# Cached GQA attention block: K turned by VectorE in 32x32 blocks, V as the moving operand, row sums by row

## The chip, the cores and the metric

The kernel runs on one core of one Trainium2 chip. The metric is device time in microseconds (us), from one launch of the whole program. A core has TensorE (PE; its weight loads are a row of their own, PEld), VectorE (DVE), ScalarE (ACT), GpSimd (POOL), SyncE (SP), which here only issues DMAs, and 16 DMA engines that all queues share.

## The reference

There are 8 batches of 4 tokens, 32 query heads over 8 key heads, 2048 cached keys for each, 128 numbers to a head, and 512 to a token. All tensors are bf16.

```python
q = (x @ wq).reshape(B, Sq, Hq, Dh).transpose(0, 2, 1, 3)
k = jnp.repeat(k_cache, rep, axis=1)      # rep = 4 query heads for a key head
v = jnp.repeat(v_cache, rep, axis=1)
scores = jnp.einsum("bhqd,bhkd->bhqk", q, k) * (Dh ** -0.5)
p = softmax(scores)
o = jnp.einsum("bhqk,bhkd->bhqd", p, v)
return o.transpose(0, 2, 1, 3).reshape(B, Sq, Hq * Dh) @ wo
```

K and V are 33.6 MB each, wq and wo 4.2 MB each: nearly all of the traffic is read once.

## The kernel before

**Units.** The work is cut into 16 units, one for each batch and each half of the key heads: four key heads (G = 4), each with 16 query rows (4 heads by 4 tokens). A unit's K is one transfer of 2 MB (`load_k`, L93) and its V another (`load_v`, L101). In SBUF a head has 32 partitions (S = 32), and each partition holds 64 consecutive keys (C = 64 chunks of 128 numbers).

**One unit's steps.**
- `transpose_part` (L168), four times a unit: PE turns 8 blocks of 128x128 fp32 words (a word is a pair of bf16 numbers) into PSUM, and DVE (parts 0 and 3) or ACT (1 and 2) copies them to the tile kt.
- `scores` (L238): 8 matmuls for each half of the keys, with q (tile q_bd) as weights of 32 columns, so that four column groups of the array work side by side.
- `maxima` (L252): DVE's maximum of each row, a shuffle that exchanges the two halves of a row, and `less`, the negated larger one.
- `exponentials` (L271): ACT's exp of the scores to s_sb, with the sum of each row in l_sb.
- `probs_to_keys` (L282): DVE turns s_sb in 32x32 blocks (tile p_t); four POOL copies, one for each key head, spread p_t into the block form `probs`, of which there are two buffers (PB = 2).
- `norms`, `sums`, `inverses` (L303 to L327), every second unit: the row sums go through a matmul with ones, and DVE takes the reciprocal of 128x128.
- `values` (L331), four quarters: 64 matmuls with V as weights (128x128) and 64 columns of probs moving, summed in one PSUM tile.
- `finish` (L344): DVE multiplies by the reciprocal and writes oT, where the head's numbers lie on partitions.

**Head and tail.** At the start q is projected: both halves (L195 to L211), then both are spread into q_bd (L212 to L230). After the last unit `to_tokens` and `to_wo_rows` bring oT to the row order in which wo was loaded, and `project` adds 32 rows of wo for each partition. wo's buffer is wq's, and it is loaded at the end, save for 256 rows (`load_wx`, L109) that come earlier in two small transfers to wx_sb; `project_few` adds them.

**Order.** The order on every engine is the order in which the program emits the instructions (`manual_schedule`). The loop (L441) runs over steps n, in which unit n's K is turned and scored, unit n-1's probabilities are spread, and unit n-2's values are computed (LAG = 2): the turn's four parts come with the spread between them, then half of the values, scores, maxima, exponentials, and the other half. K and V have three buffers each (KB, VB). SP's queue holds the loads in one order (K of a unit, then V of two units before), and each waits for its buffer: K's for the last transpose that reads it, V's for the last value matmul.

Of the kernel before, what the change touches and what calls it, by code (L numbers as in the profile page):

```python
# [14 lines left out]
def kernel(  # L15
# [23 lines left out]
    NT, J = 4, C // 8  # L39
    HP = 8  # L40
    WR = 8
    XE, XR = 4, 8
    XP, XN = 64, 2 * XE * 4 * XR
    MR = WR - XN // 128
    NP = Hq // HP
    NW = MR + (NP - 1) * WR
# [7 lines left out]
    assert Dh == 128 and C == 64 and J == 8 and HQ == 16 and NU == 16 and T == 32  # L54
# [10 lines left out]
    psum_k = ctx.enter_context(tc.tile_pool(name="psum_k", bufs=2, space=bass.MemoryType.PSUM))  # L65
    psum_s = ctx.enter_context(tc.tile_pool(name="psum_s", bufs=1, space=bass.MemoryType.PSUM))
    psum_o = ctx.enter_context(tc.tile_pool(name="psum_o", bufs=1, space=bass.MemoryType.PSUM))
    psum_l = ctx.enter_context(tc.tile_pool(name="psum_l", bufs=1, space=bass.MemoryType.PSUM))

    order = ctx.enter_context(tc.manual_schedule())  # L70

# [4 lines left out]
    q_bd = const.tile([128, Hkv // G, 2, G, B, 2, HQ], BF16, name="q_bd")  # L76
    probs = [const.tile([128, C // 2, G, HQ, 2], BF16, name=f"probs{i}") for i in range(PB)]
    ident = const.tile([128, 128], BF16, name="ident")
    ident4 = const.tile([128, 128], FP32, name="ident4")
    ones = const.tile([128, 128], FP32, name="ones")  # L80
    by_gq = const.tile([128, G, HQ], FP32, name="by_gq")
    oT = [const.tile([128, HP, 2, B, Sq], BF16, name=f"oT{n}") for n in range(2)]
    oP = [const.tile([128, MR + WR, T], BF16, name="oP0"), const.tile([128, WR, 2, T], BF16, name="oP1")]
    oX = const.tile([XP, XR, T], BF16, name="oX")
    wx_sb = const.tile([XP, XR, D], BF16, name="wx_sb")
    nat_sb = const.tile([2 * T, XP * XR + HP * 128 - XN], BF16, name="nat_sb")
# [22 lines left out]
    def load_wx(h):  # L109
        few = XN // 2  # L110
        rows = wo[h * few : (h + 1) * few, :].rearrange("(b a r) j -> a b (r j)", a=XE, r=XR)
        q0 = h * XP // 2
        nc.sync.dma_start(wx_sb[q0 : q0 + 4 * XE, :, :].rearrange("q r j -> q (r j)"), rows)

    def load_wo(p, r0, n):
        if p == 0:
            rows = wo[XN : HP * 128, :].rearrange("(q r) j -> q r j", r=MR)
        else:
            rows = wo[p * HP * 128 : (p + 1) * HP * 128, :].rearrange("(q r) j -> q r j", r=WR)
        w0 = first_row(p) + r0  # L120
        nc.sync.dma_start(wo_sb[:, w0 : w0 + n, :], rows[:, r0 : r0 + n, :])

    def first_row(p):
        return 0 if p == 0 else MR + (p - 1) * WR
# [5 lines left out]
    for u in range(2, NU + 2):  # L130
        if u < NU:
            loads.append(("k", u))
        loads.append(("v", u - 2))
        if u in (6, 12):
            loads.append(("w", u // 12))
    loads.reverse()

    def load_ready(nk, nv):
        while loads:
            kind, u = loads[-1]  # L140
            if kind == "w":
                load_wx(u)
            elif u >= (nk + KB if kind == "k" else nv + VB):
                return
            else:
                (load_k if kind == "k" else load_v)(u)
            loads.pop()

    load_ready(0, 0)

    make_identity(nc, ident4[:])
    make_identity(nc, ident[:])
    nc.vector.memset(q_bd[:, :, :, :, :, :, :], 0.0)
    for pr in probs:
        nc.gpsimd.memset(pr[:, :, :, :, :], 0.0)  # L155
    nc.gpsimd.memset(ones[:, :], 1.0)
    nc.gpsimd.memset(wx_sb[:, :, :], 0.0)
    nc.gpsimd.memset(nat_sb[:, :], 0.0)
    nc.vector.tensor_reduce(
        out=by_gq[:, :, :],  # L160
        in_=ident4[:, :].rearrange("p (g c q) -> p g q c", g=G, c=2),
        axis=AX,
        op=ADD,
    )

    kt = {}

    def transpose_part(u, t):  # L168

        k4 = ks[u][:, :, :].rearrange("s c d -> s (c d)").bitcast(FP32)  # L170
        if t % 2 == 0:
            kt[(u, t // 2)] = ktpool.tile([128, 2 * J, 128, 2], BF16, tag="kt", name="kt")
        kp = psum_k.tile([128, J, 128], FP32, tag="k", name="kp")
        for j in range(J):
            w = (t * J + j) * 128
            nc.tensor.transpose(kp[:, j, :], k4[:, w : w + 128], ident4[:, :])  # L176
        j0 = (t % 2) * J
        (nc.scalar.copy if t in (1, 2) else nc.vector.tensor_copy)(  # L178
            out=kt[(u, t // 2)][:, j0 : j0 + J, :, :].rearrange("k j s e -> k (j s e)"),
            in_=kp[:, :, :].rearrange("k j s -> k (j s)").bitcast(BF16),  # L180
        )

    for t in range(NT):
        transpose_part(0, t)

    xtp = psum_o.tile([128, R, T], BF16, tag="o", name="xtp")
# [5 lines left out]
    q_nats = []  # L194
    for hq in range(Hkv // G):  # L195
        psq = psum_k.tile([128, rep * Dh], FP32, tag="k", name="psq")
# [10 lines left out]
        q_nat = small.tile([128, rep, 2, 2, Dh // 2], BF16, tag="p_t", name="q_nat")  # L207
        halves = psq[:, :].rearrange("t (h k e) -> t h e k", h=rep, e=2)
        nc.scalar.mul(out=q_nat[:, :, :, 0, :], in_=halves, mul=scale)  # L209
        nc.vector.tensor_scalar_mul(out=q_nat[:, :, :, 1, :], in0=halves, scalar1=scale)  # L210
        q_nats.append(q_nat)  # L211
    for hq in range(Hkv // G):  # L212
        for e in range(2):
            pse = psum_k.tile([128, rep, G, B, Sq], FP32, tag="k", name="pse")
            for h in range(rep):
                nc.tensor.matmul(  # L216
                    pse[:, h, :, :, :].rearrange("d g b s -> d (g b s)"),
                    lhsT=q_nats[hq][:, h, e, :, :].rearrange("t c k -> t (c k)"),
                    rhs=ident[:, :],
                    start=True,  # L220
                    stop=True,
                )
            for c in range(2):
                rows = slice(c * 64, (c + 1) * 64)
                (nc.scalar.copy if c else nc.vector.tensor_copy)(
                    out=q_bd[rows, hq, e, :, :, c, :].rearrange(
                        "d g b (h s) -> d (g b) h s", h=rep
                    ),
                    in_=pse[rows, :, :, :, :].rearrange("d h g b s -> d (g b) h s"),
                )  # L230

    wo_sb = wpool.tile([128, NW, D], BF16, tag="w", name="wo_sb")
# [5 lines left out]
    def scores(u, tp):  # L238
        hq, b = units[u]
        if tp == 0:  # L240
            s_pss[u] = psum_s.tile([128, 2, 2 * J, S], FP32, tag="s", name="s_ps")
        for e in range(2):
            for g in range(G):
                nc.tensor.matmul(  # L244
                    s_pss[u][g * 32 : (g + 1) * 32, tp, :, :],
                    lhsT=q_bd[:, hq, e, g, b, :, :],
                    rhs=kt[(u, tp)][:, :, g * S : (g + 1) * S, e],
                    start=(e == 0),
                    stop=(e == 1),
                )  # L250

    def maxima(u):  # L252
# [5 lines left out]
            in_=s_pss[u][:, :, :, :].rearrange("q t j s -> q (t j s)"),  # L258
            axis=AX,
        )  # L260
        nc.vector.stream_shuffle(swapped[:, :], top[:, :], [i ^ HQ for i in range(32)])
# [9 lines left out]
    def exponentials(u):  # L271
        s_sbs[u] = small.tile([128, 2 * J, S, 2], BF16, tag="s_sb", name="s_sb")
# [9 lines left out]
    def probs_to_keys(u):  # L282
        p_t = small.tile([128, 2 * J * 2, HQ, 2], BF16, tag="p_t", name="p_t")
        nc.vector.transpose(  # L284
            p_t[:, :, :, :].rearrange("s x q j -> s (x q j)").bitcast(FP32),
            s_sbs[u][:, :, :, :].rearrange("q a s j -> q (a s j)").bitcast(FP32),
        )
        by_gpsimd = nc.gpsimd.tensor_copy
        copies = [by_gpsimd] * G
        if u == NU - 1:  # L290
            copies = [nc.vector.tensor_copy, nc.vector.tensor_copy, nc.scalar.copy, by_gpsimd]
        for g in reversed(range(G)):
            rows = slice(g * S, (g + 1) * S)
            to = probs[u % PB][rows, :, g, :, :].rearrange("s x q j -> s x (q j)")
            of = p_t[rows, :, :, :].rearrange("s x q j -> s x (q j)")
            if copies[g] == nc.vector.tensor_copy:
                to, of = to.bitcast(FP32), of.bitcast(FP32)
            copies[g](out=to, in_=of)  # L298

    w_gqs = {}  # L300
    r_sbs = {}

    def norms(u):  # L303
        w_gqs[u] = small.tile([128, 2, NQ], FP32, tag="w_gq", name="w_gq")
        for i in range(2):
            nc.vector.tensor_scalar_mul(  # L306
                out=w_gqs[u][:, i, :],
                in0=by_gq[:, :, :].rearrange("k g q -> k (g q)"),
                scalar1=l_sbs[u + i][:, 0:1],
            )  # L310

    def sums(u):
        l_ps = psum_l.tile([128, 2 * NQ], FP32, tag="l", name="l_ps")
        nc.tensor.matmul(  # L314
            l_ps[:, :],
# [212 lines left out]
```

## Time and profile before

| | |
|---|---|
| time, 3 runs | 188.5 us median (187.68 to 192.32) |
| time of the profiled execution | 187.17 us |
| its span, first to last instruction | 185.2 us |
| mean granted PE clock | 0.962 of full speed |
| busy: PE, DVE, ACT, POOL | 134.7, 97.5, 89.1, 76.2 us |
| DMA traffic | 75.84 MB, 410 GB/s over the span |
| K transposes on PE (L176) | 512, 69.7 us busy |
| their copies (L178) | 32 on ACT of 1868 ns, 32 on DVE of 1225 ns |
| copies to probs on POOL (L298) | 61 of 1039 ns |
| DVE transposes to p_t (L284) | 16 of 706 ns |

A row of groups gives line, engine, operation, output and inputs, shape, count, then busy time and mean duration, and the idle time before with what ended it. A row of the timeline starts with the start and the duration in us; in brackets stands the idle time before it and the instruction that ended it. Busy shares are means over the whole span: what a step is worth is read from what ends the last wait there. Times of matmuls are pipelined, so a group's duration in the timeline says more than the mean of one.

### The profile page before, as it was taken

What the parts mean: (1) busy time and instruction counts of PE and PEld (TensorE: products, weight loads), DVE (VectorE), ACT (ScalarE), POOL (GpSimd) and SP (SyncE); (2) the same over time, 40 slices, a digit from 0 to 9 for tenths busy, and PEclk for the clock granted to TensorE, in tenths of its full rate; (3) what the DMA queues carried; (4) which work ended last, traced back from release to release, by engine and by line L of the source; (5) the groups of instructions that cost most, each with busy time, mean ns of one, the idle gap of its engine ahead of it and who ended that gap; (6) DMA issues with size and microseconds to landing.
All of it is one profiled execution on the core that took longest, in us unless ns stands there. A gap on an engine that the chain in (4) does not pass through costs nothing.

```text
span 185.2 us, 4496 instructions
## 1 busy us (share of the span) xinstructions
PE 134.7 (73%) x1982; PEld 107.2 (58%) x1982; DVE 97.5 (53%) x168; ACT 89.1 (48%) x78; POOL 76.2 (41%) x74
## 2 busy tenths in 40 slices
PE   0192969669798988976786869488878686876871
PEld 0192338358686767764665667467756474655750
DVE  4022177396477738746663657445845566366300
ACT  2034244663938466393637364573737363634100
POOL 8990000817346281735262608071535335352000
PEclk9998556999999999999999999999999999999999
DMA  6999999999999999999999999999999999999980
GB/s 191 481 418 393 435 432 425 428 439 428 428 425 428 439 412 435 428 425 435 432 419 435 428 428 430 425 442 414 435 425 428 435 425 432 425 428 411 425 321 14
DMA packets 6107, 75.84 MB, mean 410 GB/s; under 512 B 712, under 2 KB 808, under 8 KB 1576
## 3 DMA queue, kind: packets, MB, share of 16 engines
q1 hardware_dynamic: 6040, 75.55, 96.2%
q8 instruction: 15, 0.25, 0.5%
q14 instruction: 4, 0.03, 0.0%
q10 hardware_dynamic: 48, 0.02, 0.0%
HBM read 75.53 MB, written 0.03 MB: 408 GB/s over the span
## 4 chain that ended last, share of the span: by engine, by line
DMA 60%; PE 19%; ACT 11%; DVE 5%; issue 2%; SPq 0%; ACTq 0%
DMA k_sb<-in_k_cache_dram 38%; PE kp L176 10%; DMA x_sb<-in_x_dram 9%; DMA v_sb<-in_v_cache_dram 8%; ACT kt L178 8%; DMA wo_sb<-in_wo_dram 6%; PE s_ps L244 4%; DVE top L256 3%; PE o_ps L336 3%; ACT s_sb L274 2%; PE psq L200 2%; DVE kt L178 1%; PE pse L216 1%; DVE less L262 0%; DVE q_nat L210 0%
## 5 line engine op out<-in xcount | busy, mean ns | idle before, releaser
L298 POOL COPY probs<-p_t 32x1024 bf16<-32x1024 bf16 x61 | 63.4, 1039 | 92.9 <-DVE p_t L284 90.4
L176 PE MATMUL kp<-ident,k_sb 128*128 128x128 f32 x512 | 69.7, 288 | 35.2 <-DMA k_sb<-in_k_cache_dram 20.3
L176 PEld LDWEIGHTS kp<-ident,k_sb 128*128 128x128 f32 x512 | 58.8, 147 | 44.4 <-issue 21.4
L178 ACT COPY kt<-kp 128x2048 bf16<-128x2048 bf16 x32 | 58.1, 1868 | 21.5 <-PE kp L176 21.5
L178 DVE COPY kt<-kp 128x2048 bf16<-128x2048 bf16 x32 | 39.2, 1225 | 47.3 <-PE kp L176 47.1
L274 ACT ACTIVATE s_sb<-s_ps,less 128x1024 bf16<-128x1024 f32 x16 | 22.4, 1400 | 49.4 <-DVE less L262 49.4
L336 PEld LDWEIGHTS <-v_sb 128*128 128x128 bf16 x1024 | 33.4, 97 | 8.7 <-issue 6.7
L336 PE MATMUL o_ps<-probs,v_sb 128*128 128x64 bf16 x1024 | 35.7, 192 | 2.0 <-DMA v_sb<-in_v_cache_dram 1.6
L256 DVE TENSOR_REDUCE top<-s_ps 128x1 f32<-128x1024 f32 x16 | 19.6, 1225 | 12.2 <-PE s_ps L244 12.2
L244 PE MATMUL s_ps<-kt,q_bd 128*32 128x512 bf16 x256 | 17.9, 396 | 0.8 <-DVE kt L178 0.8
L284 DVE STREAM_TRANSPOSE p_t<-s_sb 128x512 f32<-128x512 f32 x16 | 11.3, 706 | 1.9 <-ACT s_sb L274 1.5
L325 DVE RECIPROCAL r_sb<-l_ps 128x128 f32<-128x128 f32 x8 | 7.7, 958 | 3.5 <-PE l_ps L314 3.4
L244 PEld LDWEIGHTS <-q_bd 128*32 128x32 bf16 x256 | 4.2, 96 | 7.1 <-DVE kt L178 5.5
L155 POOL MEMSET probs<- 128x4096 bf16 x2 | 7.0, 3512 | 0.0
L423 PE MATMUL out_ps<-wo_sb,oP 128*32 128x256 bf16 x60 | 4.3, 273 | 1.4 <-DMA wo_sb<-in_wo_dram 1.4
L346 DVE TENSOR_TENSOR oT<-o_ps,r_sb 128x64 bf16<-128x64 f32 x16 | 3.5, 216 | 2.3 <-PE o_ps L336 2.3
L423 PEld LDWEIGHTS <-oP 128*32 128x32 bf16 x60 | 2.9, 96 | 2.4 <-issue 2.2
L314 PE MATMUL l_ps<-w_gq,ones 128*128 128x128 f32 x16 | 3.2, 281 | 1.3 <-DVE w_gq L306 1.3
L209 ACT ACTIVATE q_nat<-psq 128x512 bf16<-128x512 f32 x2 | 1.2, 597 | 6.2 <-PE psq L200 6.2
L200 PE MATMUL psq<-wq_sb,xT_sb 128*32 128x512 bf16 x32 | 3.6, 629 | 0.3 <-DVE xT_sb L193 0.3
L262 DVE TENSOR_SCALAR less<-swapped,top 128x1 f32<-128x1 f32 x16 | 3.4, 214 | 0.6
L216 PE MATMUL pse<-ident,q_nat 128*128 128x128 bf16 x16 | 2.4, 302 | 1.7 <-DVE q_nat L210 0.9
(45 smaller groups left out, 46.3 us busy)
## 6 DMA issues: line engine op xcount, KB each, us to landing
k_sb<-in_k_cache_dram SPq DMA_DIRECT2D x16, 2048.0 KB, 22.2
v_sb<-in_v_cache_dram SPq DMA_DIRECT2D x15, 2048.0 KB, 25.6
wq_sb<-in_wq_dram SPq DMA_DIRECT2D x1, 4096.0 KB, 17.0
wo_sb<-in_wo_dram SPq DMA_DIRECT2D x2, 1024.0 KB, 21.1
v_sb<-in_v_cache_dram SPq DMA_DIRECT2D x1, 1536.0 KB
wo_sb<-in_wo_dram SPq DMA_DIRECT2D x4, 256.0 KB, 17.8
wo_sb<-in_wo_dram SPq DMA_DIRECT2D x1, 768.0 KB, 17.1
v_sb<-in_v_cache_dram SPq DMA_DIRECT2D x1, 512.0 KB, 15.7
```

Of the source, the lines that this page charges most:

```text
L155: nc.gpsimd.memset(pr[:, :, :, :, :], 0.0)
L176: nc.tensor.transpose(kp[:, j, :], k4[:, w : w + 128], ident4[:, :])
L178: (nc.scalar.copy if t in (1, 2) else nc.vector.tensor_copy)(out=kt[(u, t // 2)][:, j0 : j0 + J, :, :].rearrange("k j s e -> k (j s e)"), ...
L200: nc.tensor.matmul(psq[g * T : (g + 1) * T, :], lhsT=xT_sb[:, r, :], rhs=wq_sb[:, r, c0 : c0 + rep * Dh], start=(r == 0), stop=(r == R - 1),)
L244: nc.tensor.matmul(s_pss[u][g * 32 : (g + 1) * 32, tp, :, :], lhsT=q_bd[:, hq, e, g, b, :, :], rhs=kt[(u, tp)][:, :, g * S : (g + 1) * S, ...
L256: nc.vector.reduce_max(out=top[:, :], in_=s_pss[u][:, :, :, :].rearrange("q t j s -> q (t j s)"), axis=AX,)
L274: nc.scalar.activation(out=s_sbs[u][:, :, :, :].rearrange("q a s j -> q a j s"), in_=s_pss[u][:, :, :, :].rearrange("q t (a j) s -> q (t a ...
L284: nc.vector.transpose(p_t[:, :, :, :].rearrange("s x q j -> s (x q j)").bitcast(FP32), s_sbs[u][:, :, :, :].rearrange("q a s j -> q (a s j ...
L298: copies[g](out=to, in_=of)
L325: nc.vector.reciprocal(r_sb[:, :], l_ps[:, :])
L336: nc.tensor.matmul(o_pss[u][:, :], lhsT=vs[u][:, 2 * (2 * a + j) + c, :], rhs=probs[u % PB][:, 2 * a + c, :, :, j].rearrange("s g q -> s ( ...
L423: nc.tensor.matmul(out_ps[half * T : (half + 1) * T, :], lhsT=left, rhs=right[:, half * DH : (half + 1) * DH], start=first, stop=last,)
```

## The change

K is no longer turned by PE. VectorE turns it, half a unit (128 partitions by 2048 words) at a time, in blocks of 32x32 words, straight from k_sb to kt. The 128 numbers of a head then stay in blocks of 32 words, and q is spread to match: for each block column k and number e of a pair, q_bd holds weights of 64 columns (four heads by 16 query rows), which are zero where head and partition don't meet. The scores of a half are 8 matmuls of 512 columns on two column groups of 64.

The exchange of halves is two copies of 64 partitions in place of the shuffle. p_t goes to probs in eight copies of 32x512 elements, four on ACT and four on POOL. The sums stay by row: two POOL copies exchange the halves, POOL adds them (`total`), and VectorE takes the reciprocal of 128x1, for every unit. The values have the probabilities of two chunks as weights and 256 numbers of V moving: 32 matmuls a unit. ACT divides them by row (`divide`), a small fp32 matmul adds the two halves and turns them (`finish`), and ACT copies the result to oT. The PSUM pools become two buffers each for scores, values and the rest. In the head, one half of q is projected, scaled and spread before the other half is begun. wo is loaded whole at the end, with no rows before, and the last part comes in pieces of 4, 2 and 2 rows.

The loop's order is new too. The core of the diff:

```diff
+    def turn_keys(u, t):
+        kts[(u, t)] = ktpool.tile([128, CT, 2, S, 2], BF16, tag="kt", name="kt")
+        nc.vector.transpose(
+            kts[(u, t)][:, :, :, :, :].rearrange("k c h s e -> k (c h s e)").bitcast(FP32),
+            ks[u][:, t * CT : (t + 1) * CT, :].rearrange("s c d -> s (c d)").bitcast(FP32),
+        )
...
+    for hq in range(Hkv // G):
+        project_q(hq)
+        spread_q(hq)
...
+    def scores(u, t):
...
+        for i in range(4):
+            k, e = i // 2, i % 2
+            for h in range(2):
                 nc.tensor.matmul(
+                    s_pss[u][h * NQ : (h + 1) * NQ, t, :, :],
+                    lhsT=q_bd[:, hq, k, e, b, :, :].rearrange("k g q -> k (g q)"),
+                    rhs=kts[(u, t)][:, h * CT // 2 : (h + 1) * CT // 2, k, :, e],
+                    start=(i == 0),
+                    stop=(i == 3),
                 )
+    def swap_halves(engine, out, in_):
+        for h in range(2):
+            engine.tensor_copy(
+                out=out[h * NQ : (h + 1) * NQ, :], in_=in_[(1 - h) * NQ : (2 - h) * NQ, :]
+            )
...
     def probs_to_keys(u):
...
+        for h in range(2):
+            for g in range(G):
+                quad = 2 * h + g // 2
+                (nc.gpsimd.tensor_copy if g % 2 else nc.scalar.copy)(
+                    out=probs[u % PB][g * S : (g + 1) * S, h, :, :, g, :],
+                    in_=p_t[quad * S : (quad + 1) * S, :, g % 2, :, :].rearrange(
+                        "s x q j -> s x j q"
+                    ),
+                )
+    def inverses(u):
...
+        swap_halves(nc.gpsimd, swapped, l_sbs[u])
+        nc.gpsimd.tensor_tensor(out=total[:, :], in0=l_sbs[u][:, :], in1=swapped[:, :], op=ADD)
+        nc.vector.reciprocal(r_sbs[u][:, :], total[:, :])
     def values(u, quarter):
...
+        t, h = quarter // 2, quarter % 2
+        for a in range(CT // 4):
+            c = quarter * C // 4 + 2 * a
             nc.tensor.matmul(
+                o_pss[u][:, :, :].rearrange("n j d -> n (j d)"),
+                lhsT=probs[u % PB][:, h, t * CT // 4 + a, :, :, :].rearrange(
+                    "s j g q -> s (j g q)"
+                ),
+                rhs=vs[u][:, c : c + 2, :].rearrange("s c d -> s (c d)"),
+                start=(c == 0),
+                stop=(c == C - 2),
+            )
+    def divide(u):
...
+            nc.scalar.mul(
+                out=o_scs[u][rows, :], in_=o_pss[u][rows, h, :], mul=r_sbs[u][rows, 0:1]
             )
     def finish(u):
...
+        nc.tensor.matmul(o_t[:, :], lhsT=o_scs[u][:, :], rhs=both[:, :], start=True, stop=True)
+        nc.scalar.copy(
...
     for n in range(NU + LAG):
         w = n - LAG
+        if 0 < n < NU:
+            turn_keys(n, 0)
         if 0 < n <= NU:
             probs_to_keys(n - 1)
+            inverses(n - 1)
         if n < NU:
             scores(n, 0)
+            if n > 0:
+                turn_keys(n, 1)
+        if w >= 1:
+            finish(w - 1)
+        if n < NU:
             scores(n, 1)
             maxima(n)
             exponentials(n)
...
         if w >= 0:
+            for quarter in range(4):
+                values(w, quarter)
+            divide(w)
```

## The prediction

> **What bounds the kernel now.** I read the page first: the span, the slices, then the costliest groups.
>
> ```profile
> span 185.2 us, 4496 instructions
> PE 134.7 (73%) x1982; PEld 107.2 (58%) x1982; DVE 97.5 (53%) x168; ACT 89.1 (48%) x78; POOL 76.2 (41%) x74
> PEclk9998556999999999999999999999999999999999
> DMA  6999999999999999999999999999999999999980
> ```
>
> The DMA row is full from the second slice to the last but one. No engine is: 75.5 MB at 425 to 435 GB/s set the time, and the engines fit inside. The timeline of one steady unit says how well they fit:
>
> ```profile
> 150.26 0.70 DVE L284 STREAM_TRANSPOSE p_t<-s_sb 128x512 f32<-128x512 f32 x1
> 151.10 4.32 POOL L298 COPY probs<-p_t 32x1024 bf16<-32x1024 bf16 x4 [5.89 <-DVE p_t L284]
> 153.62 1.05 PE L244 MATMUL s_ps<-kt,q_bd 128*32 128x512 bf16 x16
> 154.72 1.23 DVE L256 TENSOR_REDUCE top<-s_ps 128x1 f32<-128x1024 f32 x1 [0.72 <-PE s_ps L244]
> 156.18 0.21 DVE L262 TENSOR_SCALAR less<-swapped,top 128x1 f32<-128x1 f32 x1
> 156.49 1.40 ACT L274 ACTIVATE s_sb<-s_ps,less 128x1024 bf16<-128x1024 f32 x1 [3.13 <-DVE less L262]
> 157.37 1.94 PE L176 MATMUL kp<-ident,k_sb 128*128 128x128 f32 x16 [1.64 <-DMA k_sb<-in_k_cache_dram]
> ```
>
> The same p_t step is at 159.62 one unit later, so a unit takes 9.7 us here, and the next unit's first matmul waits 1.64 us for K's DMA. Early on, with K there ahead, the chain of waits shows units 8.1 us apart (VectorE's maximum at 44.85, 52.96, 61.06). So this kernel's engines have 1.6 us to spare in each unit. POOL's four copies begin 0.14 us after p_t and take 4.3 us, but nothing on VectorE waits for POOL. That is what the change alters.
>
> **The loop after the change.** It removes 512 fp32 transposes of PE (69.7 us), their 64 evictions (58.1 us on ACT, 39.2 on DVE), the sums on PE and 16 matmuls of the extra wo rows, all under the DMA today. It adds 32 transposes of 128x2048 words on VectorE. Its queue now reads: first half of K's turn, p_t, the reciprocal, second half of the turn, maximum, two swaps, less. The reciprocal waits for POOL's total, and POOL does four copies to probs, two swaps and the addition first, the copies starting only after p_t. So VectorE stands at the reciprocal for POOL's whole leg; behind it stand the second turn, for it the second half of the scores, and for those the next maximum. I go round once, from the end of a unit's scores (us):
> - maximum to less: 0.06 to the start, 1.23 (L256), two swaps 0.30 (the shuffle of 128x1 takes 0.15), less 0.21, two gaps of 0.04: 1.88.
> - first turn. The nearest row is p_t: 512 words in 0.706. Not shown is 2048. The line through p_t and the maximum (1024 words in 1.225) rises by 1.01 ns a word and gives 2.26; four times p_t is 2.82; with the slope of POOL's memset (4096 in 3.51, 0.86 ns each) it is 2.03. I take 2.31, just over the line, since p_t is the same operation. 0.03 + 2.31, to 4.22. ACT's exponential (1.40 + 0.18) ends at 3.6, under it.
> - p_t 0.03 + 0.71: 4.96.
> - POOL: 0.14 to the start, then four copies of 32x512. 1024 elements take 1.04; half is 0.52, and the instruction's price at worst is not halved, 1.04. I take 0.56, by elements and a little fixed cost: 2.24, to 7.34. ACT makes the other four copies beside them (1.04 for 1024, so 0.6 each).
> - two swaps and an addition of one element on POOL: no such row; its shortest memsets take 0.11 and the 128-element select 0.295. 0.35 to 0.9 for the three; I take 0.55, to 7.89. Back to DVE 0.10, reciprocal of one element 0.20 (128 take 0.96): 8.19.
> - second turn 0.03 + 2.31: 10.53.
> - half the scores: eight matmuls of 512 columns, two column groups at once, so four in a row. Four groups of four in a row took 1.05 above and, at the granted clock of 0.5, 1.90 (the 16 at 26.55 in the head). PE would be idle some 4 us before this step, and the head shows what that does:
>
> ```profile
> 14.00:16.00 2.00, 1.09 (x8) 0.86 (x8) 0.66 (x1) 1.92 (x2) 0.00 (x0) 1.00 0.83 360
> 16.00:18.00 2.00, 0.00 (x0) 0.00 (x0) 0.56 (x1) 0.00 (x0) 0.00 (x0) 0.90 0.95 401
> 18.00:20.00 2.00, 1.28 (x16) 0.65 (x20) 0.22 (x1) 0.00 (x0) 0.00 (x0) 0.50 0.99 426
> 30.00:32.00 2.00, 2.00 (x13) 1.82 (x12) 1.64 (x3) 1.70 (x3) 0.00 (x0) 0.69 1.06 442
> ```
>
> (Columns: busy PE, PEld, DVE, ACT, POOL; then granted clock, DMA share, GB/s.) PE's last matmul ended at 15.3; a clock of 0.90 over 16 to 18 means half speed from about 17.6; it came back only near 31, after five unbroken busy us. So this half of the scores costs 1.05 to 1.90, or 3.4 if the two groups also don't overlap. I take 1.65, nearer the slow end: 12.2 with the 0.06 before it.
>
> One unit is 12.2 us (10.7 with every term low, 15.7 with every term high), so the DMA, at 9.7, is no longer the bound: K and V wait for buffers, which VectorE and PE free late. The new values (32 matmuls of 256 columns) run right after the scores: L423's 24 matmuls of 256 columns in pairs took 1.64, so 0.137 each, and the scores' slope of 0.215 per 512 gives 0.107: 3.4 to 4.4 at full clock, some 5.5 when they start at half. p_t ends at 4.96 and POOL's second pair of copies, which needs them done, starts at 6.2, so they are covered; beyond 6.2 each 0.1 counts.
>
> **Head.** x still lands at 18.4; the first xT copy ends at 18.97. The first projection's 16 matmuls end at 20.9 (half of L200's 3.6). Then four scalings in a chain, DVE and ACT in turn at 0.69 and 0.60 (L210, L209): 23.8. Four spreads of 0.6 with two PSUM buffers and copies of 0.58 to 0.69 (L225): the buffer is free at 26.6. Only then the second projection (1.8), its scalings (2.9) and spreads (2.6): 34.05. Two halves of the first scores at half clock, 3.6: 37.6. Before, they ended at 28.4. K0's turn, 4.6 us after its landing at 8.6, is hidden under x, and so are POOL's memsets (7.0 for probs, by size 3.5 for the two q_g), done near 12. The old order, both projections first and spreads after, had no such chain.
>
> **Tail.** After unit 15's scores: values of 13 to 5.0, their division (two ACT copies of some 0.28) and the fp32 matmul to 6.0; values of 14 to 9.9, division and matmul to 10.9; values of 15 to 14.6, division, matmul and copy to 15.8. Tokens, copies and row turns (8 + 8 small matmuls, 0.63, 0.58, 0.68, 0.43 in the old tail, with the first projection of 1.1 between) to 18.3; 48 matmuls at 0.068 to 21.7; copy 0.37; then 3.3, as from 181.9 to the old end: 25.8 with gaps. wo has landed by then: V15's buffer comes free one unit earlier, and 15 us of transfers follow it. The 256 wo rows that went in two transfers of 0.13 MB between K and V (SP's queue, L113) now go with the rest: 0.6 us of transfer, moved from one place to another and covered in both.
>
> **Sum.** 37.6 + 15 x 12.2 + 25.8 = 246.4 of span. The profiled run took 187.17 for a span of 185.2, so 2.0 more: 248.4 against its 187.2, forecast 248. The median of the runs shown is 188.5, 0.7% above the profiled one, less than my terms are sure of. The unit's ends give 226 and 301 by the same sum.
>
> **Rivals.**
> - *The clock stays low through the values too.* For: 4 to 5 us of idleness in each unit, and the head's slow recovery. Against: scores and values in one piece are over 5 us busy. Scores 1.90, values 6.9 (32 x 0.213), and POOL's second pair waits 0.75: 13.2 a unit, 37.6 + 198 + 26.5 + 2.0 = 264.
>
> The Trainium skill (TensorE: Matmul & The Clock Gate, Part 1: The HAM clock gate) says half clock follows an idle window of some 3.4 us and full clock a busy one of as much. The trace shows half clock sooner, 2.3 us after the last matmul, and a later return. By the page's figure for the return the values would warm up half-way, which is the forecast, not this rival.
>
> - *POOL's copies cost by instruction,* 1.04 each for half the elements: 14.1 a unit, 277. Against: its memsets go with size.
> - *POOL's leg doesn't hold VectorE* (total is ready when asked for): 12.2 - 3.03 = 9.2 a unit, 37.6 + 138 + 25.8 + 2.0 = 203. Against: copies stand ahead of the swaps in POOL's queue.
> - *VectorE keeps up, not slower.* Place: the same wait at the reciprocal. If it is gone and turns (2.03) and scores (1.05) sit at their low ends, a unit is 8.0 and the DMA is the bound again. It decides from about 8.3 a unit, where the late start is caught up. K4 is asked for at 43 to 45, when the earlier transfers end at about 42; K15 lands 2 us later than before's 157.3, its scores end 6.6 later, 24 of tail: 190 + 2.0 = 192.
>
> **How the numbers follow.** Forecast 0.62 (own range 232 to 262), low clock 0.14, POOL's price 0.10, no hold 0.08, keeps up 0.06. Range 218 to 274: it leaves out the last two and most of POOL's price, about 0.2. Two per cent is about what a measurement of this kernel tells from no change: the DMA alone needs today's time, so faster 0.02 and same 0.04, both out of the last rival; slower 0.94.
>
> **What would show it.** Right: VectorE idle some 3 us before each reciprocal, ended by POOL; turns of 2.3 us; maxima 12 us apart; DMA slices of 7 or 8 tenths; first scores ending near 37; PEclk below 9 in the loop. Wrong: turns near 1.2, idle at the reciprocal below 1 us, or DMA slices still full. Over 13 us a unit, the clock and POOL's copies are to be read first.

## The result

The changed kernel takes 250.6 us (median of 4 runs, 250.0 to 252.1); the kernel before took 188.1 us beside it. The ratio is 1.3365, 95% interval 1.3285 to 1.3444. Some runs on these chips are disturbed and some 2 to 4% longer; ratios here compare undisturbed runs alone. The profiled execution took 250.01 us for a span of 248.2.

The page of the kernel after, its span, engines and DMA row:

```profile
span 248.2 us, 2569 instructions
PE 144.5 (58%) x964; PEld 91.0 (37%) x964; DVE 117.7 (47%) x140; ACT 86.2 (35%) x160; POOL 59.1 (24%) x124
PEclk9999996555968778968778867768867768877999
DMA  7999999397998979998979998979997909199500
```

The DMA row has holes from the eighth slice on, and no engine is above 58%. So neither the transfers nor any engine's amount of work looks like the bound: the loop waits within itself. The chain of work that ended last, read in order of time over one unit, says where (start, duration in us, what; steps of under 0.1 us are left out):

```profile
122.04 1.93 PE s_ps L209 x8
124.00 1.24 DVE top L227
125.25 0.15 DVE swapped L219
125.42 0.16 DVE swapped L219
125.60 0.21 DVE less L233
125.81 2.22 DVE kt L139
128.03 0.60 DVE p_t L255
...
128.78 0.60 POOL probs L262
...
130.73 0.62 POOL probs L262
131.40 0.18 POOL l_swapped L219
131.62 0.19 POOL l_swapped L219
131.88 0.20 POOL l_total L276
132.11 0.16 DVE r_sb L277
132.27 2.22 DVE kt L139
134.53 1.88 PE s_ps L209 x8
136.44 1.24 DVE top L227
```

Every step begins within 0.15 us of the end of the one before it. One unit is a single file: PE, VectorE, POOL, VectorE, PE. From the first maximum (36.57) to the last (223.54) are 15 units of 12.46 us. The waits, summed over the span (us in total, times, longest), put numbers on the two places where VectorE stands:

```profile
...
ACT s_sb L245 <- DVE less L233: 94.1, 16, 7.2
...
PE s_ps L209 <- DVE kt L139: 72.0, 17, 4.9
DVE r_sb L277 <- POOL l_total L276: 56.0, 16, 3.6
DVE top L227 <- PE s_ps L209: 32.3, 16, 2.7
```

VectorE is idle for 56.0 us before the reciprocals and for 32.3 before the maxima: 5.5 us of each unit. The first two rows belong to engines that wait for VectorE in their turn. And what the new instructions cost, among the groups (mean ns after the busy time):

```profile
L262 POOL COPY probs<-p_t 32x512 bf16<-32x512 bf16 x64 | 38.7, 605 | 168.6 <-DVE p_t L255 139.0
L139 DVE STREAM_TRANSPOSE kt<-k_sb 128x2048 f32<-128x2048 f32 x32 | 73.4, 2296 | 6.2 <-DMA k_sb<-in_k_cache_dram 6.2
L277 DVE RECIPROCAL r_sb<-l_total 128x1 f32<-128x1 f32 x16 | 2.6, 164 | 56.0 <-POOL l_total L276 56.0
```

The longest idle time on VectorE stands before one of its shortest instructions, a reciprocal of 164 ns.

### The profile page after: what moved, and what is told of

Its sections match the earlier page's. It is cut to its first block, busy times and chain, and to the rows that moved or that the text cites. A ratio compares the mean times of both kernels' runs of the same rounds, so it can differ in the third digit from the quotient of the medians.

```text
span 248.2 us, 2569 instructions
## 1 busy us (share of the span) xinstructions
PE 144.5 (58%) x964; PEld 91.0 (37%) x964; DVE 117.7 (47%) x140; ACT 86.2 (35%) x160; POOL 59.1 (24%) x124
## 4 chain that ended last, share of the span: by engine, by line
DVE 40%; PE 27%; POOL 15%; DMA 7%; issue 7%; ACT 2%; SPq 0%; POOLq 0%; ACTq 0%; DVEq 0%
DVE kt L139 25%; PE s_ps L209 13%; POOL probs L262 12%; PE o_ps L288 9%; DMA x_sb<-in_x_dram 7%; DVE top L227 6%; DVE p_t L255 3%; POOL l_swapped L219 2%; DVE swapped L219 2%; PE psq L159 2%; PE out_ps L354 2%; POOL l_total L276 1%; PE pse L180 1%; DVE less L233 1%; DVE q_g L173 1%
## 5 line engine op out<-in xcount | busy, mean ns | idle before, releaser
L209 PE MATMUL s_ps<-kt,q_bd 128*64 128x512 bf16 x256 | 49.1, 519 | 72.0 <-DVE kt L139 72.0
L262 POOL COPY probs<-p_t 32x512 bf16<-32x512 bf16 x64 | 38.7, 605 | 168.6 <-DVE p_t L255 139.0
L288 PE MATMUL o_ps<-v_sb,probs 128*128 128x256 bf16 x512 | 77.1, 324 | 0.0
L139 DVE STREAM_TRANSPOSE kt<-k_sb 128x2048 f32<-128x2048 f32 x32 | 73.4, 2296 | 6.2 <-DMA k_sb<-in_k_cache_dram 6.2
L288 PEld LDWEIGHTS <-probs 128*128 128x128 bf16 x512 | 58.4, 117 | 24.5 <-issue 9.9
L209 PEld LDWEIGHTS <-q_bd 128*64 128x64 bf16 x256 | 18.0, 132 | 89.0 <-issue 78.6
L262 ACT COPY probs<-p_t 32x512 bf16<-32x512 bf16 x64 | 39.4, 615 | 4.2 <-DVE p_t L255 2.7
L227 DVE TENSOR_REDUCE top<-s_ps 128x1 f32<-128x1024 f32 x16 | 19.6, 1224 | 32.3 <-PE s_ps L209 32.3
L302 ACT ACTIVATE o_sc<-o_ps,r_sb 64x128 f32<-64x128 f32 x32 | 11.6, 362 | 27.1 <-PE o_ps L288 26.9
L309 PE MATMUL o_t<-both,o_sc 128*128 128x64 f32 x32 | 7.0, 299 | 2.6 <-ACT o_sc L302 2.6
L219 POOL COPY l_swapped<-l_sb 64x1 f32<-64x1 f32 x32 | 5.8, 180 | 1.6
```

The source lines that it names most:

```text
L139: nc.vector.transpose(kts[(u, t)][:, :, :, :, :].rearrange("k c h s e -> k (c h s e)").bitcast(FP32), ks[u][:, t * CT : (t + 1) * CT, :].r ...
L209: nc.tensor.matmul(s_pss[u][h * NQ : (h + 1) * NQ, t, :, :], lhsT=q_bd[:, hq, k, e, b, :, :].rearrange("k g q -> k (g q)"), rhs=kts[(u, t) ...
L219: engine.tensor_copy(out=out[h * NQ : (h + 1) * NQ, :], in_=in_[(1 - h) * NQ : (2 - h) * NQ, :])
L227: nc.vector.reduce_max(out=top[:, :], in_=s_pss[u][:, :, :, :].rearrange("q t c s -> q (t c s)"), axis=AX,)
L262: (nc.gpsimd.tensor_copy if g % 2 else nc.scalar.copy)(out=probs[u % PB][g * S : (g + 1) * S, h, :, :, g, :], in_=p_t[quad * S : (quad + 1 ...
L288: nc.tensor.matmul(o_pss[u][:, :, :].rearrange("n j d -> n (j d)"), lhsT=probs[u % PB][:, h, t * CT // 4 + a, :, :, :].rearrange("s j g q ...
```

## The experiments

The theory: VectorE, which takes its instructions in order, is held at the reciprocal by POOL's copies, and the second turn of K, the scores and the next maximum stand behind it; PE's half clock adds to it. The rivals: late buffers and transfers, the amount of POOL's work, the amount of VectorE's work. Each kernel below is the changed kernel with the edit shown.

**1. The sums before the copies.** POOL does the same work in another order.

```diff
             s_sbs[u][:, :, :, :].rearrange("q a s j -> q (a s j)").bitcast(FP32),
         )
+        inverses(u)
         for h in range(2):
...
             probs_to_keys(n - 1)
-            inverses(n - 1)
```

> POOL exchanges and adds the row sums before its four copies of p_t instead of after them; nothing else moves, the reciprocal keeps its place in VectorE's queue. Theory (VectorE is held at the reciprocal by POOL's copies): the 3.5 us of idleness before each reciprocal go to under 0.3, the unit falls from 12.46 to about 8.6 to 9.0, K's transfers are the bound again, and the time is about 194 us (190 to 203). Rival 1 (the loop is held by late buffers of K and V, or by the number of POOL's copies): POOL does as much work as before, so no more than 10 us of gain, 240 to 250. Rival 2 (PE's half clock is what costs): the clock is set by PE's own work, about 235 to 250.

196.2 us (195.5 and 196.9; the kernel before took 188.4 beside it): 54 us gone by moving three POOL instructions of together 0.7 us ahead of four others. VectorE's timeline in one unit of it:

```profile
104.80 0.21 DVE L233 TENSOR_SCALAR less<-swapped,top 128x1 f32<-128x1 f32 x1
104.93 2.30 DVE L139 STREAM_TRANSPOSE kt<-k_sb 128x2048 f32<-128x2048 f32 x1
107.16 0.67 DVE L255 STREAM_TRANSPOSE p_t<-s_sb 128x512 f32<-128x512 f32 x1
107.75 0.12 DVE L278 RECIPROCAL r_sb<-l_total 128x1 f32<-128x1 f32 x1
107.79 2.29 DVE L139 STREAM_TRANSPOSE kt<-k_sb 128x2048 f32<-128x2048 f32 x1
111.92 1.23 DVE L227 TENSOR_REDUCE top<-s_ps 128x1 f32<-128x1024 f32 x1 [1.84 <-PE s_ps L209]
```

The reciprocal has no idle time before it. The maxima here are at 103.20 and 111.92, 8.7 us apart; the next follows 8.1 later, with half the scores in 1.08 instead of 1.75 us. PE's waits before the scores are shorter (34.5 us over the run in place of 72.0), and the mean granted clock is 0.885 in place of 0.80. The unit is now under the 9.7 us in which K and V arrive, and late in the run VectorE waits for K's transfer again. Rival 1 allowed 10 us. Rival 2 allowed a gain, but not this one: the part that the clock can explain is tested by itself in 3.

**2. More work for POOL on the way.** 

```diff
+        nc.gpsimd.memset(idle_sb[:, :], 0.0)      # 128 x 1024, bf16
         swap_halves(nc.gpsimd, swapped, l_sbs[u])
```

> A POOL memset of 1024 elements into a tile that nothing reads, by the memsets of the profile 0.9 us, between POOL's copies and the exchange of the sums. Theory: every unit pays it in full, 15 x 0.9 = 13.5, about 264 us, and the idleness before the reciprocal grows by 0.9. Rival (POOL is busy a quarter of the span and its leg is covered by DMA or PE): within 2 us of 250.6.

265.9 us (one run), 15.4 more than 250.6. The waits for the total:

```profile
DVE r_sb L279 <- POOL l_total L278: 72.9, 16, 5.1
```

The memset takes 0.95 us with 0.06 of gap, and the idle time before the reciprocals is 72.9 us in place of 56.0, 1.06 for each. POOL is busy only 28% of this span, and yet each microsecond added to it here counts in full.

**3. PE kept busy.** 

```diff
+        if 0 < n < NU:
+            keep_busy(16)        # 16 matmuls of 256 columns into a PSUM tile that nothing reads
         if n < NU:
             scores(n, 1)
```

> Sixteen matmuls of 256 columns, whose result nothing reads, stand on PE's queue before the second half of each unit's scores, where PE waited 4 us. Theory on the clock (half the scores ran at half speed because of that wait): the granted clock in the loop goes from about 0.77 to above 0.95, half the scores from 1.92 to about 1.05, and 15 x 0.87 = 13 us are gained, about 237 us. Rival (the scores' 1.92 us come from two column groups that don't overlap at any clock): no gain, 250 us, or a few us lost where the added matmuls end late.

241.0 us (one run): 9.6 of the 13 expected. The mean clock is 0.92 in place of 0.80. PE's timeline of one unit:

```profile
124.90 1.91 PE L274 MATMUL d_ps<-q_bd,ident 128*128 128x256 bf16 x16
130.09 1.10 PE L209 MATMUL s_ps<-kt,q_bd 128*64 128x512 bf16 x8 [3.28 <-DVE kt L139]
131.12 3.67 PE L300 MATMUL o_ps<-v_sb,probs 128*128 128x256 bf16 x32
```

The same half of the scores that took 1.93 takes 1.10, about the 1.05 that four groups took for as many matmuls in a row before the change, so two groups of 64 columns do overlap and the rest was the clock. It didn't hold in every unit (the wait before the maxima fell from 32.3 to 23.7 us, 0.54 a unit and not 0.87). PE still waits 3.28 us for the turn: the clock is the smaller part of the loop.

**4. More work for VectorE in the wait.**

```diff
             probs_to_keys(n - 1)
+            if n < NU:
+                extra_turn(n)    # 128 x 2048 words of K into a tile that nothing reads
             inverses(n - 1)
```

> A third transpose of 128x2048 words in each unit, into a tile that nothing reads, on VectorE's queue between p_t and the reciprocal. Theory (VectorE only waits there): 15 x 2.3 = 35 us more of VectorE's busy time, the idleness before the reciprocal goes from 3.5 to 1.2, and the time stays within 2 us of 250.6. Rival (the amount of VectorE's work, two long turns a unit, is what bounds the loop): 15 x 2.3 = 35 us more, about 285 us.

251.0 us (one run), with 32.9 us more of VectorE's busy time (150.6 against 117.7). The waits for the total:

```profile
DVE r_sb L284 <- POOL l_total L283: 23.2, 16, 3.6
```

23.2 us instead of 56.0: the added turns went into the wait and cost 0.4 us together. The amount of VectorE's work is not the bound here; the place of the wait in its queue is.

**5. More work for POOL off the way.** The memset of 2, behind the copies, in the kernel with the sums first.

> The row sums ahead of POOL's copies, and the memset of 1024 elements (0.95 us) behind the copies. Theory (POOL costs only where VectorE waits for it): 15 x 0.95 us more of POOL's work cost nothing here, within 2 us of the 196.2 of the kernel with the sums first. Rival (POOL's amount of work counts): about 14 us more, 210.

195.7 us (one run), against 196.2 without it. The same instruction that cost 15 us in 2 costs nothing that shows here: VectorE no longer waits for POOL's total (no such wait is left in its trace).

**6. The rest: the late start.** In the kernel with the sums first, the second half of q is projected in step 3 and spread in step 4 of the loop, not before it. For that the two q_g have buffers of their own, and wo's buffer, which is wq's, is taken only at the end.

> The row sums ahead of POOL's copies, and besides only the first half of q is projected and spread before the loop; the second half, which units 8 to 15 need, follows in steps 3 and 4 of the loop. Theory (with the wait gone, what is left over the kernel before is the late start of the loop, which lets the transfers run dry once, and the longer tail): the first scores end near 29 instead of 36.5, K4 is asked for before the earlier transfers are done, the DMA row has no hole, and the time is 188 to 192 us against 196. Rival (the loop of 8 to 9 us a unit is itself too slow for the transfers): no more than 2 us of gain over 196.

Undisturbed runs took 190.2 and 190.5 us; the ratio to the kernel before is 1.0169 (1.0145 to 1.0193). The first scores end at 29.3 us in place of the 36.4 of kernel 1, so most of the 8 us that were left came from the head: 6 by the two times, 5 if each kernel is taken against the kernel before that ran beside it (188.4 and 187.2 us). What is not as expected is a hole in the transfers. GB/s in 40 slices:

```profile
GB/s 215 445 444 403 438 410 434 441 438 420 424 438 438 434 413 432 122 424 424 431 434 434 427 427 431 431 431 434 434 420 438 427 434 417 438 425 415 418 261 7
```

It falls to 122 in the seventeenth slice, at 75 to 80 us. The next V was asked for only at 77.4 us, when the values that held its buffer had ended. They stood on PE behind the spread of q, from 71.3 us, and took 6.05 us, most of them at half clock (0.50 over 70 to 75 us).

**7. All of it, with PE kept busy.** 

```diff
-        if w >= 1:
+        if w >= 1 and n < NU:
             finish(w - 1)
+        if 0 < n < NU:
+            keep_busy(16)
...
             divide(w)
+        if n >= NU:
+            finish(w - 1)
```

> As the kernel with late q, and in the last steps the small fp32 matmul that finishes a unit stands behind the next unit's values instead of ahead of them, and sixteen matmuls of 256 columns that nothing reads stand before each second half of the scores. Theory: two gaps of 1.2 us in the tail go, and values and scores of the last unit run at full clock (1.2 and 0.9 us): 185 to 190 us, level with the kernel before, since its transfers alone end 4 us before its end. Rival: the added matmuls delay the values and the tail stays, 190 or more.

193.6 us, ratio 1.0333 (1.0295 to 1.0372): slower than without. The tail itself is shorter, 21.4 us from the last maximum to the end (170.93 to 192.3) against 23.1. The loss is elsewhere. GB/s in 40 slices:

```profile
GB/s 208 446 436 399 385 385 388 395 388 388 378 388 388 392 388 387 385 388 402 426 436 426 426 433 423 436 433 429 429 433 426 433 433 426 426 418 429 423 283 10
```

From 19 to 87 us the transfers ran at 378 to 395, with the DMA row full, where the kernel of 6 had 403 to 441 up to its hole. In the first 30 us the two kernels issue the same instructions, and the lower rate is there from 19 us on, so the added matmuls don't begin it. The kernels of 1 to 4 and the changed kernel show the same rate in parts of their head. By an estimate from this row, those 67 us would be some 61 at 430 GB/s, which is more than the 3 us that this kernel loses against 6. What sets the rate is open, and only one of the four runs has a profile; that the added matmuls cost nothing is not shown either.

**8. The tail, without added matmuls.** As 6 and the diff of 7 without `keep_busy`; the late half of q is scaled and copied by ACT alone, in steps 3 and 5 (the same edit stands at the copies to q_bd).

```diff
-            if g % 2:
+            if g % 2 or hq:
                 nc.scalar.mul(out=to, in_=of, mul=scale)
```

> As the kernel with late q (190.2 us), but without added matmuls: the second half of q is scaled and copied by ACT alone, in steps 3 and 5, so that VectorE does not stand there, and in the last steps the fp32 matmul that finishes a unit stands behind the next unit's values. Theory: the one hole in the DMA row (122 GB/s in one slice, about 3.4 us) goes and the tail is 2.3 us shorter; the transfers then end as in the kernel before, and 186 to 189 us result, level with its 187.2, not below 185. Rival (VectorE's turns of 4.6 us a unit keep the last unit late whatever the rest does): 190 or more.

Undisturbed runs took 185.9 and 186.2 us beside 187.1 to 187.5 of the kernel before: ratio 0.9934 (0.9913 to 0.9956). That is 0.7% less, under the two per cent that the prediction takes a measurement of this kernel to tell from no change: level with the kernel before. Its page:

```profile
span 184.5 us, 2568 instructions
DMA  6998999999999999999999999999999999999980
```

The DMA row is full from end to end, as before the change. That ACT's part in this closed the hole is not shown: one unit still takes 12.4 us (maxima at 72.99 and 85.38), and a V is asked for 15 us after the one before it, but that is a step later, and the transfers asked for by then last. The tail is 21.9 us, 1.2 shorter and not 2.3. At the very end PE waits for the last pieces of wo:

```profile
179.47 1.03 PE L353 MATMUL out_ps<-wo_sb,oP 128*32 128x256 bf16 x12 [0.16 <-DMA wo_sb<-in_wo_dram]
180.74 0.40 PE L353 MATMUL out_ps<-wo_sb,oP 128*32 128x256 bf16 x4 [0.25 <-DMA wo_sb<-in_wo_dram]
```

So the turn on VectorE fits under the transfers once POOL's queue is in the right order, the head is short and the tail doesn't trail. There is then little more to gain from it, since the transfers fill the row with either way of turning K.

## Why the prediction was right, step by step

| step | predicted us | measured us |
|---|---|---|
| end of the first scores | 37.6 | 36.5 |
| maximum to less | 1.88 | 1.84 |
| a turn of 2048 words | 2.31 | 2.30 |
| p_t | 0.71 | 0.67 |
| four copies of POOL | 2.24 | 2.56 |
| two swaps and the addition | 0.55 | 0.73 |
| to VectorE, reciprocal | 0.30 | 0.20 |
| half the scores | 1.65 | 1.93 |
| one unit | 12.2 | 12.46 |
| tail after the last scores | 25.8 | 24.7 |
| span | 246.4 | 248.2 |

The total is nearer than its parts, and that much is luck: 15 units of 12.46 are 4.0 us longer than the sum had them, and the head and the tail are 1.1 shorter each. Within the unit, POOL's leg and the scores were sized low by 0.8 together. Some 0.4 of it came back since in the chain a turn takes 2.22 us and p_t 0.60, each beginning before the one ahead of it has ended, and 0.1 at the reciprocal.

- *The wait at the reciprocal* was the right step: 3.48 us idle in a unit, ended by POOL, against 3.03 for POOL's whole leg in the sum. Kernels 1, 2, 4 and 5 show it from four sides: taken away, lengthened, filled, and moved off the way.
- *The turn* was right to 0.01: the line through p_t and the maximum, 2.26, was nearer than either end.
- *POOL's leg*: its copies and its sums were sized low by 0.5. Half the elements took 0.605 and not 0.56, with 0.04 between copies, and three instructions of one element took 0.73.
- *The clock* was taken between its ends, and lay at the slow one: 1.93 where 1.90 was the bound. Kernel 3 shows that full speed was to be had in most units, and that this is worth 9.6 us. The rival with values at half clock too didn't come: it had 6.9 us for them, and they took 4.2 to 5.7 in the loop, so PE warmed on the way. POOL's and ACT's copies hid them, but for 0.1 us in one unit (3.58 of idle time before the reciprocal in place of 3.48). The granted clock in the unit shown is 0.50 from 122 to 126 and 1.00 from 128.
- *The head* ended 1.1 early. Half of that is the chain of spreads and copies, which let the scores begin at 33.5 and not 34.05; the other half is the scores, 3.0 us in place of 3.6, whose second part no longer ran at half speed. Its size, 8 us more than before, was right, and in 6 it gave back 5 to 6.
- *The rivals.* POOL's price by instruction was wrong (605 ns for half of what took 1039). That POOL's leg doesn't hold VectorE was wrong here and is what kernel 1 makes true; I gave it 203, it is 196.2: its units are 8.87 us on average in place of 9.2, with half the scores in 1.1 us in many of them, and its first scores end 1.2 earlier. The last rival's place was right, its condition too narrow: it needed shorter turns, where kernel 8 reaches the transfers' time with turns of 2.30 by starting and ending earlier.
- *A reading.* The two p_t steps from which the prediction takes 9.7 us for a unit before the change, 150.26 and 159.62, are 9.36 apart. The maxima there, 154.72 and 164.41, are 9.7 apart, so the figure stands; the sum doesn't use it.

## What to carry to other kernels

When an engine takes its instructions in order, a result of 0.2 us that comes from a slower neighbour can hold up everything queued behind it: ask of each new cross-engine wait what stands ahead of its producer and what stands behind its consumer. Go once round the loop and add up the single file before trusting shares of busy time; here no engine was above 58% and the kernel was a third slower. A probe that puts work into the gap, beside one that puts it on the way, tells a wait from a load in two runs.

## What the runs showed of the hardware that was not expected

The granted clock reads 1.00 in the head of the changed kernel, from 17 to 34 us, while 16 matmuls of the projection take 1.90 us, about as long as where the profile before shows 0.50 (32 in 3.60). In this head, durations tell the clock better than the row.

In the unit shown, PE's last matmuls before its two waits end at 117.8 and 130.8 us. The granted clock is 0.74 over 120 to 122 and 0.66 over 134 to 136, which puts its fall to half at 121.0 and 134.6: 3.2 and 3.8 us after the last matmul, against 2.3 in the head before. It is 0.55 over 126 to 128, so it came back near 127.8, some 5.8 us after PE had begun at 122.04. The Trainium skill (TensorE: Matmul & The Clock Gate, Part 1: The HAM clock gate) gives a window of some 3.4 us that runs free of the kernel. The falls here lie about it, and the return is later than one window.

From 512 words (672 ns) to 2048 (2296 ns), VectorE's transposes in 32x32 blocks take 1.06 ns for each further word. In the unit shown p_t begins 2.22 us after the turn ahead of it, 0.07 before that turn's 2.30 are over.
